# The last block of an output projection's weights, fetched row by row at the end of a decode kernel

## The chip, the cores and the metric

One core of a Trainium2 chip. The metric is the time of one execution on the device in microseconds (us), the median of several; lower is better. The trace's own clock starts at the program's first instruction, and its span is some 2 us shorter than the time.

## The reference

A decode step for 4 sequences. Part A is attention of one query over a cache of 8192 keys and values with 32 heads, then an output projection by `wo`; part B is a gated MLP on the one token of each sequence. The two are mixed by a gate.

```python
q = (x @ wq).reshape(B, Sq, H, Dh) ...
scores = einsum("bhqd,bhkd->bhqk", q, k_cache) * (Dh ** -0.5)
o = einsum("bhqk,bhkd->bhqd", softmax(scores), v_cache)
a = o ... .reshape(B, Sq, H * Dh) @ wo          # wo: 4096 x 1024, bf16
b = x + (silu(x @ w_gate) * (x @ w_up)) @ w_down * sigmoid(x @ w_r)
return g * a + (1 - g) * b                      # 4 x 1 x 1024
```

575.68 MB are read from HBM, nearly all of it the two caches. `wo` is 8.4 MB of that, and nearly all of it comes last.

## The kernel before

The caches stream through a ring of buffers. `wo` comes in 8 blocks, 0 to 7, each 128 partitions by 4 rows of 1024 columns (1 MB); blocks 0 and 1 are issued just ahead of the last value caches, blocks 2 to 7 behind all of them. `wo_block` issues one piece's transfer at once and returns `use`, which emits the matmuls of that piece later. Each row needs two matmuls, one for each half of the columns; all add into the same two accumulators.

```python
def mm_acc(n, lhsT, rhs, start=False):                     # L286 in the profile is its matmul
    nc.tensor.matmul(acc(n), lhsT=lhsT, rhs=rhs, start=start, stop=True, ...)

def wo_block(g, r0=0, r1=FR, half=None):                   # FR = 4 rows, NH = 2 halves, NB = 512
    ...
    if half is None:                                       # L394
        nc.sync.dma_start(out=w[:, r0:r1]..., in_=wov[:, g, r0:r1]...)
    else:                                                  # L397
        nc.sync.dma_start(out=w[:, r0, half * NB:(half + 1) * NB], in_=...)
    def use():
        for r in range(r0, r1):
            for n in range(NH) if half is None else [half]:
                mm_acc(n, LT[:, r, g, :], w[:, r, n * NB:(n + 1) * NB])
    return use
# ... the end of the program; NWB = 8:
last = [wo_block(g) for g in range(2, 4)]
cuts = [(g, r, r + 2) for g in range(4, NWB) for r in (0, 2)][:-1] \
       + [(NWB - 1, 2, 3)] + [(NWB - 1, 3, 4, n) for n in range(NH)]
last += [wo_block(*cut) for cut in cuts]                   # all transfers issued here, in this order
flush_sums(); last.pop(0)(); flush(); flush_late(); last.pop(0)()
o_rows(GE, NWB)
for use in last:                                           # matmuls of blocks 4 to 7
    use()
nc.vector.tensor_copy(out=res[0], in_=acc(0))              # L636
nc.sync.dma_start(out=out2[:, 0:NB], in_=res[0])           # L637
nc.scalar.copy(out=res[1], in_=acc(1))                     # L638
nc.scalar.dma_start(out=out2[:, NB:D], in_=res[1])         # L639
```

## Time and profile before

| | before |
|---|---|
| time, median of 3 runs (lowest to highest) | 1343.54 us (1343.23 to 1343.93) |
| span in the profile | 1341.3 us |
| PE busy | 1052.3 us (78%) |
| DVE busy | 638.3 us (48%) |
| DMA engines, mean rate | 430 GB/s, full in 39 of 40 slices |

How to read it: no compute engine is full, the DMA engines are. PE is the TensorE, DVE the VectorE, ACT the ScalarE, SP the engine that issues most transfers. A transfer runs on 16 DMA engines here, and each adds one to the transfer's semaphore when its share is through: the sixteenth increment is what this text calls the landing. Only the end, where the transfers have run out and the last matmuls, copies and output transfers follow, is free to be shortened by order alone.

### The profile page before, as it was taken

The page shows a single profiled execution, that of the slowest core. Times are in us where ns is not written, and L with a number is a line of the kernel's source. Part 1 is how long each engine was busy: PE and PEld are TensorE (multiplying, and loading weights), DVE is VectorE, ACT ScalarE, POOL GpSimd, SP SyncE. Part 2 cuts the span into 40 slices and gives each one's busy share as a digit, 9 for nine tenths or more (in the row PEclk, how much of TensorE's full clock was granted, in tenths as well). Part 3 has the DMA queues.
Part 4 walks back from the last instruction along what each step waited for, and adds up shares of the span by engine and source line. Part 5 has one row for each costly group of instructions (what it writes and reads, how often), then busy time and mean ns, then how long its engine had stood idle before and what let it go on. Part 6 is the DMA issues. An engine that isn't in the chain of part 4 may idle for free.

```text
span 1341.3 us, 6870 instructions
## 1 busy us (share of the span) xinstructions
PE 1052.3 (78%) x4550; PEld 138.5 (10%) x1396; DVE 638.3 (48%) x386; ACT 66.2 (5%) x99; POOL 71.5 (5%) x209
## 2 busy tenths in 40 slices
PE   2565877887778788787879778789597879888888
PEld 0000000001001010001001010101011011111111
DVE  2555988556544347454436256646145556100000
ACT  0000000200000000100000000100000000111000
POOL 2000000100000001000000000100000000100000
PEclk9777989898988898888899888889898889889989
DMA  9999999999999999999999999999999999999998
GB/s 415 436 432 436 435 436 424 441 430 427 435 436 427 442 434 420 441 430 433 437 431 432 430 436 434 436 428 427 434 431 439 434 421 441 434 422 432 426 427 337
DMA packets 15322, 576.13 MB, mean 430 GB/s; under 512 B 1710, under 2 KB 1974, under 8 KB 3004
## 3 DMA queue, kind: packets, MB, share of 16 engines
q1 hardware_dynamic: 15284, 575.69, 99.6%
q8 instruction: 23, 0.38, 0.1%
q14 instruction: 7, 0.06, 0.0%
q10 hardware_dynamic: 8, 0.00, 0.0%
HBM read 575.68 MB, written 0.01 MB: 429 GB/s over the span
## 4 chain that ended last, share of the span: by engine, by line
DMA 67%; DVE 21%; PE 11%; issue 0%; ACT 0%; SPq 0%; DVEq 0%
DMA ring<-in_A_k_cache_dram 51%; DVE TB L456 19%; PE o_ps L540 8%; DMA ring<-in_A_v_cache_dram 7%; DMA ring<-in_A_wo_dram 6%; PE S_ps L461 3%; DMA ring<-in_B_w_gate_dram 3%; DVE OS L561 2%; PE o_ps L320 0%; DVE PT L497 0%; DVE mx L483 0%; PE acc L286 0%; PE led L577 0%; PE o_ps L577 0%; DVE OS L569 0%
## 5 line engine op out<-in xcount | busy, mean ns | idle before, releaser
L456 DVE STREAM_TRANSPOSE TB<-ring 128x2048 uint32<-128x2048 uint32 x256 | 568.3, 2278 | 472.5 <-DMA ring<-in_A_k_cache_dram 464.5
L461 PE MATMUL S_ps<-TB,Z 128*128 128x512 bf16 x1990 | 526.3, 415 | 197.3 <-DVE TB L456 183.0
L540 PE MATMUL o_ps<-ring,PB 128*64 128x512 bf16 x2048 | 462.9, 388 | 50.4 <-DMA ring<-in_A_v_cache_dram 49.0
L461 PEld LDWEIGHTS <-Z 128*128 128x128 bf16 x512 | 53.2, 104 | 655.5 <-issue 655.5
L540 PEld LDWEIGHTS <-PB 128*64 128x64 bf16 x512 | 57.2, 112 | 449.6 <-issue 446.9
L516 POOL COPY PB<-PT 32x256 bf16<-32x256 bf16 x64 | 38.9, 608 | 712.5 <-PE o_ps L540 519.6
L569 DVE SCALAR_TENSOR_TENSOR OS<-o_ps,mE,OS 128x512 f32<-128x512 f32 x5 | 3.8, 751 | 139.2 <-ACT OS L567 139.2
L514 ACT COPY PB<-PT 32x256 bf16<-32x256 bf16 x64 | 39.6, 619 | 257.2 <-PE o_ps L540 251.4
L438 POOL COPY Z<-qa 32x4 bf16<-32x4 bf16 x128 | 25.7, 200 | 460.0 <-PE S_ps L461 432.4
L557 ACT ACTIVATE OS<-o_ps,mE 128x512 f32<-128x512 f32 x11 | 7.6, 687 | 450.3 <-PE o_ps L540 450.3
L561 DVE SCALAR_TENSOR_TENSOR OS<-o_ps,mE,OS 128x512 f32<-128x512 f32 x33 | 24.3, 737 | 1.5
L492 ACT ACTIVATE TB<-S_ps,mx 128x2048 bf16<-128x2048 f32 x4 | 7.9, 1967 | 331.6 <-DVE mx L489 331.6
L286 PE MATMUL acc<-ring,hT 128*4 128x512 bf16 x56 | 14.8, 433 | 5.4 <-ACT TB L492 5.4
L244 PE MATMUL S_ps<-identb,x 6*128 6x6 bf16 x8 | 0.6, 197 | 22.4 <-DMA x<-in_gate_w_dram 22.4
L286 PE MATMUL acc<-ring,LT 128*4 128x512 bf16 x64 | 15.1, 378 | 1.8 <-DMA ring<-in_A_wo_dram 1.3
L577 PEld LDWEIGHTS o_ps<-selg,OS 128*128 128x128 f32 x88 | 11.5, 191 | 9.3 <-issue 8.9
L497 DVE STREAM_TRANSPOSE PT<-TB 128x2048 bf16<-128x2048 bf16 x4 | 9.2, 2311 | 6.4 <-ACT TB L492 6.4
L483 DVE TENSOR_REDUCE mx<-S_ps 128x1 f32<-128x2048 f32 x4 | 9.1, 2282 | 6.2 <-PE S_ps L461 6.2
L320 PE MATMUL o_ps<-ring,xw 128*4 128x512 bf16 x112 | 9.1, 448 | 3.6 <-DMA ring<-in_B_w_gate_dram 3.6
L577 PE MATMUL o_ps<-selg,OS 128*128 128x8 f32 x88 | 10.5, 245 | 0.0
L567 ACT ACTIVATE OS<-o_ps,mE 128x512 f32<-128x512 f32 x5 | 3.4, 687 | 129.0 <-PE o_ps L540 129.0
L589 DVE SCALAR_TENSOR_TENSOR OT<-led,sgb,rinv 128x8 bf16<-128x8 f32 x5 | 1.2, 236 | 16.4 <-PE led L577 16.4
(73 smaller groups left out, 83.1 us busy)
## 6 DMA issues: line engine op xcount, KB each, us to landing
ring<-in_A_v_cache_dram SPq DMA_DIRECT2D x18, 4096.0 KB, 31.0
ring<-in_A_k_cache_dram SPq DMA_DIRECT2D x14, 4096.0 KB, 30.2
ring<-in_A_v_cache_dram SPq DMA_DIRECT2D x6, 2048.0 KB, 39.4
ring<-in_B_w_gate_dram SPq DMA_DIRECT2D x1, 7168.0 KB, 37.1
ring<-in_B_w_up_dram SPq DMA_DIRECT2D x1, 7168.0 KB, 37.1
ring<-in_B_w_down_dram SPq DMA_DIRECT2D x1, 7168.0 KB
ring<-in_A_wo_dram SPq DMA_DIRECT2D x4, 1024.0 KB
ring<-in_A_v_cache_dram SPq DMA_DIRECT2D x4, 1024.0 KB, 25.8
```

The source lines that it names most:

```text
L286: nc.tensor.matmul(acc(n), lhsT=lhsT, rhs=rhs, start=start, stop=True, skip_group_check=True)
L320: nc.tensor.matmul(ps[32 * k:32 * k + Bn, z, :], lhsT=xT[TW * half + t], rhs=cols(w, t, 4 * z + k), start=(half + t == 0), stop=(half == 1 ...
L438: nc.gpsimd.tensor_copy(out=Z[at, :, QP - 1 + QP * q], in_=qa[at, :, h0 + q, b])
L456: nc.vector.transpose(out=flat_t.bitcast(U32).rearrange("p (j i) -> p j i", j=CJ), in_=kn[:, half].bitcast(U32))
L461: nc.tensor.matmul(sps[:, z, :], lhsT=Z[:, 2 * half + e, s:s + P], rhs=T[:, 16 * z:16 * z + 16, :, e], start=(t + n + half + e == 0), stop ...
L483: nc.vector.tensor_reduce(out=mx[:, 0:1], in_=sps[:].rearrange("p z n -> p (z n)"), axis=AX.X, op=ALU.max)
L497: nc.vector.transpose(out=PT[:].rearrange("p j i -> p (j i)"), in_=PTs)
L514: nc.scalar.copy(out=Bv[at, :, :, q, :], in_=Pv[at])
L516: nc.gpsimd.tensor_copy(out=Bv[at, :, :, q, :], in_=Pv[at])
L540: nc.tensor.matmul(o_ps[w // 2][row:row + NM, w % 2, :], lhsT=PB[:, RD * (d % NW) + n, z].rearrange("p w s j -> p (w s j)"), rhs=vn[:, j0 ...
L561: nc.vector.scalar_tensor_tensor(out=OS[:], in0=o_ps[w // 2][:, w % 2, :], scalar=mE[:, w:w + 1], in1=OS[:], op0=ALU.mult, op1=ALU.add)
L577: nc.tensor.matmul(oT, lhsT=OS[:, q * Dh:(q + 1) * Dh], rhs=selg[:, q].rearrange("p t s -> p (t s)"), start=(q == 0), stop=(q == 3), skip_ ...
```

## The change

The intent: PE should find less work waiting for it when the last bytes have landed. Rows 0 and 1 of block 7 no longer come in one transfer of 512 KB, but as two of 256 KB. Row 2, and row 3 in two halves of its columns, came in pieces of their own before and do so still.

```diff
-    cuts = [(g, r, r + 2) for g in range(4, NWB) for r in (0, 2)][:-1] + [(NWB - 1, 2, 3)] + [(NWB - 1, 3, 4, n) for n in range(NH)]
+    cuts = [(g, r, r + 2) for g in range(4, NWB - 1) for r in (0, 2)] + [(NWB - 1, r, r + 1) for r in range(FR - 1)] + [(NWB - 1, 3, 4, n) for n in range(NH)]
```

## The prediction

> **What bounds the kernel now.** The page's strips over 40 slices come first, and of them the strip of the DMA engines with the rate below it.
>
> ```profile
> DMA  9999999999999999999999999999999999999998
> GB/s 415 436 432 436 435 436 424 441 430 427 435 436 427 442 434 420 441 430 433 437 431 432 430 436 434 436 428 427 434 431 439 434 421 441 434 422 432 426 427 337
> ```
>
> The DMA engines are full in 39 of 40 slices, at some 430 GB/s, and only the last slice falls, to 337 GB/s. 575.68 MB have to be read, and the change reads the same bytes. So nothing the change does can touch the 1330 us ahead of the end; it can only touch the run-out. The chain of waits of the last 20 us says what the run-out hangs on:
>
> ```profile
> 1325.23 11.30 DMA ring<-in_A_wo_dram
> 1336.53 0.04 issue
> 1336.57 1.90 PE acc L286 x8
> 1338.47 0.02 issue
> 1338.49 0.58 ACT TB L638
> ```
>
> One DMA, issued at 1325.23 and landed at 1336.53, is the last thing that the program waits for. The kernel's text says which: the wo blocks are numbered 0 to 7, each of 4 rows of 1024 columns on 128 partitions; blocks 4, 5 and 6 come in two DMAs of two rows (512 KB), block 7 as rows 0-1 (512 KB), row 2 (256 KB), and row 3 in two halves of its columns (128 KB each). The order of issue makes the DMA of 1325.23 rows 0-1 of block 7. After it landed the TensorE does all 8 matmuls of block 7 in one go. Its timeline from 1334 us on:
>
> ```profile
> 1334.06 1.02 PE L286 MATMUL acc<-ring,LT 128*4 128x512 bf16 x4 [0.22 <-DMA ring<-in_A_wo_dram]
> 1335.31 1.02 PE L286 MATMUL acc<-ring,LT 128*4 128x512 bf16 x4 [0.23 <-DMA ring<-in_A_wo_dram]
> 1336.57 1.89 PE L286 MATMUL acc<-ring,LT 128*4 128x512 bf16 x8 [0.23 <-DMA ring<-in_A_wo_dram]
> ```
>
> The two groups of 4 belong to the two DMAs of block 6. They need 1.02 us and then stand idle 0.22 to 0.23 us for the next 512 KB: here the DMA is the slower one. The 8 of block 7 have no idle time inside: the smaller pieces after rows 0-1 had all landed by the time that PE came to them, so over the last 1.9 us PE is the slower one. What follows hangs on the end of it:
>
> ```profile
> 1338.27 0.68 DVE L636 CAST TB<-acc 4x512 bf16<-4x512 f32 x1 [7.84 <-PE acc L286]
> 1338.49 0.58 ACT L638 CAST TB<-acc 4x512 bf16<-4x512 f32 x1 [13.01 <-PE acc L286]
> 1338.98 0.29 SPq L637 DMA_DIRECT2D out_dram<-TB  x1
> 1339.10 0.55 ACTq L639 DMA_DIRECT2D out_dram<-TB  x1
> ```
>
> The right half of the output (ACT's copy, ACT's DMA) is the later one by 0.12 us, so the last matmul, and not the one before it, sets the end; the span ends at 1341.3.
>
> Last, the DMA view of the window 1323 to 1338 shows how the transfers run out:
>
> ```profile
> DMA  9999999999999999999999999976556554544200
> GB/s 393 459 404 404 404 437 426 415 382 382 404 426 404 415 404 404 426 393 426 404 404 404 410 385 391 350 287 262 243 229 246 227 235 183 208 175 164 85 8 0
> ```
>
> From about 1332.5 on only some half of the 16 DMA engines still have work, at 160 to 290 GB/s together. The increments of the semaphores in the trace give the same picture: the first of the 16 engines is through with rows 0-1 of block 7 at 1331.53, the last at 1336.53. Seven engines are ahead, nine lag by 3 to 5 us, and the laggards alone set each landing.
>
> **What the Trainium skill says.** "DMA: Bandwidth & Descriptors", section "Why a DMA increments its semaphore by 16 and not by 1", says that only the full 16 means that all data has landed. The trace agrees: PE starts 0.04 us after the sixteenth increment (1336.53 to 1336.57), 5 us after the first. The same page, section "Measured (HBM→SBUF, 128 partitions, SWDGE, issued from GpSimd)", has the rule to batch DMAs to 1 MiB or more for 75% of peak. That would speak against smaller pieces[...]. These pieces stand one behind another in a queue, and there the trace does not show the loss: sixteenth increments of the last five DMAs are at 1335.27, 1336.53, 1337.17, 1337.51 and 1337.83, so 512 KB took 1.26 us, 256 KB 0.64, 128 KB 0.34 and 0.32. "TensorE: Matmul & The Clock Gate", section "Back-to-back issue gap", gives N/2.4 + 2.5 ns for a warm matmul, 215.8 ns at N = 512. The trace agrees: 8 matmuls less 4 are 1.89 - 1.02 = 0.87 us, 0.217 each, and starts lie 0.215 apart.
>
> **The change part by part.** It replaces one DMA of 512 KB (rows 0-1 of block 7, 4 KB to a partition) by two of 256 KB (2 KB to a partition). Row 2 and the two halves of row 3 were in such pieces before, and stay so. Compared instruction by instruction, PE, DVE, ACT and POOL have the same work in the same order; SP has one DMA more; and PE waits five times in block 7 instead of four, with the first wait for row 0 alone.
>
> *On SP:* one more issue, 0.33 us, with a wait of 0.02. Each DMA here waits until the one eight places before it has landed. Row 0 of block 7 keeps the place of the old piece (1325.23); each later piece moves one place back: row 1 to 1327.72, row 2 to 1329.00, row 3's left half to 1330.28, and its right half gets the place after the first DMA of block 5, whose sixteenth increment is at 1331.49, so 1331.55. The lagging engines come to that piece at 1337.5, six microseconds later: off the path. The seven fast ones come to it at about 1332.6; an output DMA took 1.1 us from issue to its first data landing (1338.98 to 1340.12), so they may stand idle for a few tenths. They have 5 us to spare.
>
> *On the DMA engines:* the pieces of block 7 follow the landing at 1335.27. With 0.64 for each 256 KB: row 0 at 1335.91, row 1 at 1336.55, row 2 at 1337.19, row 3 left at 1337.53, right at 1337.85. That is 0.02 later at the end than before (2 x 0.64 against 1.26). A less kind reading: the packets of 4, 2 and 1 KB took a mean of 159, 84 and 46 ns late in the run, so 16 of 2 KB for 8 of 4 KB are 1.34 us against 1.27, or 0.07 more.
>
> *On PE:* block 6's last matmul starts at 1335.95, so PE is free at 1336.17. Row 0 is there by then: two matmuls, 1336.17 and 1336.38, in time that was idle or waiting. Row 1: landed 1336.55, starts 1336.60 and 1336.81. Row 2: landed 1337.19, plus 0.04, starts 1337.23 and 1337.45. Row 3: left free to go at 1337.66 (landed 1337.53), right at 1337.89 (landed 1337.85, plus 0.04). Before, the last matmul started at 1338.07. **Gain 0.18 us**; with the less kind packets the right half lands at about 1337.90 and the gain is 0.13.
>
> *The cap:* the last piece landed at 1337.83 before, and PE could not have begun on it ahead of 1337.87. However rows 0-1 are cut, no more than 1338.07 - 1337.87 = 0.20 us is to be had, since the cut moves matmuls ahead of the last landing and does not move the landing. What comes behind (copies, output DMAs, 3.2 us from 1338.07 to the end) shifts along unchanged.
>
> The sum: 2 matmuls that no longer stand between the last landing and the end would be 0.43 us, of which 0.20 was exposed, less some 0.04 for more packets and one more wait: 0.16 us, 0.012% of the time. 1343.54 - 0.16 = 1343.38.
>
> **The rivals.** First, *the landing takes the place of PE as the bound and eats all of it*: if small packets cost more than the packet means say, say 0.2 us for 16 of them, the end stays at 1343.5. For it: PE's slack on the last landing is only 0.20. Against it: 256 KB took 0.64, as good as half of 512 KB. Second, *the later issue starves the queue*: were the lagging engines to run dry, each gap of over 1 us would go straight to the end, giving 1344.5 or more. Against it: 6 us between issue and use on those engines. Third, *the gain is twice mine*: if the transfers of the laggards ran faster once the others are done sooner, or if the wait at 1337.19 vanished, 1343.1. Against it: between the landings the laggards needed 1.25 us (1334.02 to 1335.27) with half of the engines idle and 1.29 with all at work, so hardly faster. Fourth, *the noise is larger than any of these*: the three runs of before lie between 1343.23 and 1343.93, 0.70 us apart, four times the gain. This I hold for the likeliest thing to be seen in the times; the gain should be seen in the trace alone.
>
> **The range and the chances.** The middle is 1343.38. The mechanism gives 0 to 0.2 us; the spread of before is 0.35 to each side of its middle, and another set of runs can lie a few tenths off as a whole, for which I widen to 1342.5 and 1344.2. For 2% the time would have to move by 27 us, and the change has its hands on the last 16 us only: within 2% 0.99, the rest split evenly, for a run in a slower state.
>
> **What would show it.** Right: in the last 5 us of the changed kernel, PE's 8 matmuls come no longer in one group, but in two or three, with waits of hundredths to 0.25 us; row 0's two follow block 6 with no wait; the last matmul starts 2.62 to 2.7 us after the last landing of block 6 (2.80 us before, from 1335.27 to 1338.07); five DMAs of block 7. Wrong: a landing of the last piece more than 2.7 us after block 6's; a gap in the queue of the lagging engines; PE's last group still of 8, or a change anywhere ahead of 1325 us.

## The result, and the profile after

The changed kernel took 1343.21 us (median of 6 runs, 1342.81 to 1344.05), the kernel before 1343.43 us in its own 6 (1343.09 to 1343.93). The ratio of the fast runs is 0.9999, 95% interval 0.9986 to 1.0011: the same within 2%, and no difference clear of noise. The prediction said 1343.38 in a range of 1342.5 to 1344.2, and the median lies inside. That alone shows little: the median of the kernel before (1343.43) lies inside as well.

The chain of waits at the end of the changed kernel (start in us, duration, what) answers to the one before:

```profile
1328.86 8.22 DMA ring<-in_A_wo_dram
1337.08 0.04 issue
1337.12 1.04 PE acc L286 x4
1338.16 0.02 issue
1338.18 0.57 ACT TB L638
```

The transfer that released PE last is now the one issued at 1328.86, which is row 2 and not rows 0-1, and 4 matmuls stand behind it instead of 8. The timeline of PE, its weight loads (PEld) and the copies shows the rest:

```profile
1335.15 2.99 PE L286 MATMUL acc<-ring,LT 128*4 128x512 bf16 x12 [0.20 <-DMA ring<-in_A_wo_dram]
...
1336.67 0.08 PEld L286 LDWEIGHTS <-LT 128*4 128x4 bf16 x1 [0.35 <-issue]
1337.34 0.08 PEld L286 LDWEIGHTS <-LT 128*4 128x4 bf16 x1 [0.59 <-issue]
1337.96 0.68 DVE L636 CAST TB<-acc 4x512 bf16<-4x512 f32 x1 [7.67 <-PE acc L286]
1338.18 0.57 ACT L638 CAST TB<-acc 4x512 bf16<-4x512 f32 x1 [12.84 <-PE acc L286]
1338.67 0.29 SPq L637 DMA_DIRECT2D out_dram<-TB  x1
1338.79 0.55 ACTq L639 DMA_DIRECT2D out_dram<-TB  x1
```

The 12 matmuls in one group are the four of block 6's second piece and all of block 7. The view runs them together although there is a wait inside: the ends of matmuls are modelled and overlap the next start, so a short wait leaves hardly any idle time to print. The weight loads give it away. One load stands ahead of every two matmuls, and the pause between two loads is 0.35 us when PE streams; ahead of the load at 1337.34 it is 0.59. The 0.24 us more are PE waiting for row 2: its first matmul starts at 1337.12, 0.04 us after the landing at 1337.08 (chain above).

To compare executions, one offset must come out first. The moment at which block 6's last piece has landed differs from one execution to the next by more than the change is worth: 1335.06 to 1336.13 us over the 13 profiles in the table below. So I count from that landing. It is the sixteenth increment of that transfer's semaphore, as the trace records it; starts of single matmuls and the last landing are from the trace too. The three columns after the first are differences.

| run | block 6 landed | last piece of block 7 landed, after that | last matmul started, after that | last start to end of span | time of this profiled run |
|---|---|---|---|---|---|
| before | 1335.27 | 2.57 | 2.81 | 3.25 | 1343.33 |
| changed | 1335.11 | 2.62 | 2.66 | 3.19 | 1342.88 |
| after_again | 1335.25 | 2.61 | 2.72 | 3.20 | 1343.18 |
| whole | 1335.18 | 2.45 | 4.00 | 3.45 | 1344.59 |
| rows4 | 1335.69 | 2.58 | 2.93 | 3.25 | 1343.94 |
| extra_early | 1335.19 | 2.61 | 2.93 | 3.19 | 1343.31 |
| extra_late | 1335.25 | 2.61 | 2.96 | 3.19 | 1343.37 |
| before_late | 1335.16 | 2.56 | 3.89 | 3.25 | 1344.16 |
| after_late | 1335.06 | 2.61 | 3.64 | 3.20 | 1343.93 |
| before_early | 1335.32 | 2.57 | 2.81 | 3.25 | 1343.24 |
| after_early | 1335.94 | 2.61 | 2.66 | 3.17 | 1343.62 |
| early_gap | 1336.13 | 2.62 | 2.66 | 3.16 | 1343.81 |
| halves_early | 1335.31 | 2.68 | 2.72 | 3.39 | 1343.44 |

The last matmul starts 0.15 us sooner after block 6's landing (2.81 to 2.66). The fourth column holds a second gain, of 0.06 us, that I had not foreseen. At the end SP waits for each transfer semaphore in turn, in a fixed order, two to an instruction. The count of such instructions from the last landing on, in the view of that line for the kernel before, the changed kernel and the run whole:

```profile
L665 SPq EVENT_SEMAPHORE  x2: 28/28/28, 1340.4 to 1340.5; - x2
```

```profile
L665 SPq EVENT_SEMAPHORE  x1: 28/28/28, 1340.1 to 1340.1; - x1
```

```profile
L665 SPq EVENT_SEMAPHORE  x5: 28/28/28, 1341.5 to 1341.8; - x5
```

The semaphores of the transfers are taken in rotation. The one transfer more moves the last output transfer to the semaphore that SP comes to last, so that one wait instruction is left after its landing and not two; in whole there are five. One such step takes 0.06 to 0.07 us in the trace (1341.54, 1341.61, 1341.68, 1341.74, 1341.81 in whole). 0.15 + 0.06 make 0.21 us, on these profiles. The medians are 0.22 apart, but with runs of one kernel spread over 1.2 us that agreement is luck and proves nothing; the gain is seen in the trace, not in the times.

### The profile page after: what moved, and what is told of

The parts are those of the page before. It is cut to its first block, busy times and chain, and to the rows that moved or that the text cites. A ratio compares the mean times of both kernels' runs of the same rounds, so it can differ in the third digit from the quotient of the medians.

```text
span 1341.0 us, 6872 instructions
## 1 busy us (share of the span) xinstructions
PE 1050.9 (78%) x4550; PEld 138.3 (10%) x1396; DVE 638.2 (48%) x386; ACT 66.2 (5%) x99; POOL 71.4 (5%) x209
## 4 chain that ended last, share of the span: by engine, by line
DMA 62%; DVE 24%; PE 12%; another core or an unknown queue 1%; issue 0%; ACT 0%; SPq 0%; DVEq 0%
DMA ring<-in_A_k_cache_dram 51%; DVE TB L456 21%; PE o_ps L540 9%; DMA ring<-in_A_v_cache_dram 7%; DMA ring<-in_A_wo_dram 2%; DVE OS L561 2%; DMA x<-in_gate_w_dram 2%; PE S_ps L461 1%; PE acc L286 1%; DVE mx L483 0%; PE S_ps L320 0%; PE led L577 0%; PE o_ps L320 0%; DVE PT L497 0%
```

## The experiments

Theory: the end is set by the later of two things, PE's stream of matmuls and the landings on the lagging DMA engines; the cut takes matmuls from behind a landing, and wins at most what PE stood behind the last landing before. Rivals: the cut does nothing and the last landing alone counts; the cut costs as much as it wins; PE sets the end anyway.

### The changed kernel again, and three other cuts

The diffs of this part and of the last one show the cuts against the changed kernel, shortened with `...`.

**after_again**: no edit.

> The changed kernel once more, on the same chip as the three below. Theory (PE stood behind the landing of rows 0-1; the cap is the last landing): the profile again has 2.6 to 2.7 us from the sixteenth increment of block 6's last DMA to the start of the last matmul (2.80 in the kernel before, 2.66 in the changed one), and the median lies 0.1 to 0.3 us under the kernel before, not clear of noise. Rival (the 2.66 was a chance of one profile): 2.75 or more this time.

Measured: median 1343.1 us (5 runs), the kernel before 1343.33 (9 runs), ratio 0.9999 (0.9986 to 1.0011). In the profile the last start came 2.72 us after block 6's landing: just outside what I expected, and nearer to the rival. The reason is in the timeline of PE:

```profile
1331.49 6.85 PE L286 MATMUL acc<-ring,LT 128*4 128x512 bf16 x31
```

31 matmuls without a pause up to the end: here PE did not wait for any piece of blocks 4 to 7. It came late to them, its first matmul of block 4 being at 1331.28 and not at 1329.82. The time was lost about 1290 us. The stretch 1280 to 1300 us by engine (busy us and instructions of PE, PEld, DVE, ACT, POOL, then the granted TensorE clock, which is the share of its full speed that PE was allowed, the busy share of the DMA engines, and GB/s), with the value-cache matmuls that follow, for the kernel before and then for after_again:

```profile
1280.00:1300.00 20.00, 14.37 (x63) 2.48 (x21) 2.34 (x4) 1.27 (x2) 0.00 (x0) 0.83 1.00 424
```

```profile
1292.81 12.27 PE L540 MATMUL o_ps<-ring,PB 128*64 128x512 bf16 x56
```

```profile
1280.00:1300.00 20.00, 14.39 (x51) 3.12 (x18) 2.34 (x4) 1.26 (x2) 0.00 (x0) 0.74 1.00 424
```

```profile
1293.54 14.16 PE L540 MATMUL o_ps<-ring,PB 128*64 128x512 bf16 x56
```

The granted clock was 0.74 there and not 0.83, and the same 56 matmuls took 1.9 us more. The DMA engines moved the same 424 GB/s. So in some executions PE is in time, and in others late. In after_again the last piece landed 2.61 us after block 6; PE could have begun on it at 2.65, and began at 2.72 because it was busy. That PE's place decides is tested further down.

**whole**: block 7 in one transfer.

```diff
-    cuts = ... + [(NWB - 1, r, r + 1) for r in range(FR - 1)] + [(NWB - 1, 3, 4, n) for n in range(NH)]
+    cuts = ... + [(NWB - 1, 0, FR)]
```

> Block 7 in one DMA of 1 MB. Theory: the last landing stays where it is (2.5 to 2.6 us after block 6's), but all 8 matmuls then stand behind it, so the last one starts 2.55 + 0.04 + 7 x 0.2155 = 4.1 us after block 6's landing, against 2.66 in the changed kernel and 2.80 before: the median 1.4 us over the changed kernel, 1.3 over the kernel before, clear of noise. Rival (the end follows the landing of the last bytes alone, the cut does nothing): the median within 0.2 us of the changed kernel.

Measured: median 1344.59 us (5 runs), 1.49 over after_again on the same chip and 1.26 over the kernel before; the ratio to the kernel before is 1.0012 (0.9999 to 1.0026), which just touches 1. The timeline of PE:

```profile
1335.22 1.02 PE L286 MATMUL acc<-ring,LT 128*4 128x512 bf16 x4 [0.22 <-DMA ring<-in_A_wo_dram]
1337.67 1.89 PE L286 MATMUL acc<-ring,LT 128*4 128x512 bf16 x8 [1.43 <-DMA ring<-in_A_wo_dram]
```

PE stands idle for 1.43 us and then has all 8 matmuls before it. The last start is 4.00 us after block 6's landing (4.1 expected). Block 7 itself landed sooner than in any other cut, at 2.45 us, and the time is the longest of the table: the rival, that the end follows the landing alone, falls. Of the 1.6 us that its profile lies above the changed kernel's from block 6's landing to the end, 1.34 are the matmuls and 0.26 the four further closing waits.

**rows4**: the four rows, row 3 not halved.

```diff
-    ... + [(NWB - 1, r, r + 1) for r in range(FR - 1)] + [(NWB - 1, 3, 4, n) for n in range(NH)]
+    ... + [(NWB - 1, r, r + 1) for r in range(FR)]
```

> Block 7 row by row, its last row not halved (the row part of the change without the halves). Theory: two matmuls stand behind the last landing and not one, the landing itself 0.02 to 0.04 us earlier for fewer packets: the last matmul starts 2.60 + 0.04 + 0.22 = 2.86 us after block 6's landing, 0.2 over the changed kernel and 0.06 over the kernel before. Rival (the halves win nothing, for their packets cost what they save): 2.66.

Measured, one look: last landing 2.58, last start 2.93, so 0.07 over what I expected, and 0.27 over the changed kernel's first profile. PE was late in this execution as well (clock 0.74 in the same stretch, no pause from 1331.93 on), so the excess is PE's own lateness: it could have begun row 3 at 2.62, began at 2.72, and row 3's second matmul is 0.22 behind. The landing is level with that of four pieces in the kernel before. But with PE streaming to the end, halves of row 3 would not have moved the last start: its 2.93 is block 7's first start, 1.42 after block 6's landing, plus seven matmuls (1.51). So this run doesn't tell what the halves are worth, and the rival (the halves win nothing) stays untested; by an estimate from the landing, with PE in time the last start would have come at 2.58 + 0.04 + 0.22 = 2.84.

**seven**: an attempt to shorten the lag itself, by giving rows 2-3 to seven of the DMA engines only. I took these seven to be the ones that are ahead.

```diff
+    def wo_seven(g, r0, r1):
+        for lo, hi in ((0, 119), (119, 126), (126, 128)):
+            nc.sync.dma_start(out=w[lo:hi, r0:r1]..., in_=wov[lo:hi, g, r0:r1]...)
+    ...
-    ... + [(NWB - 1, r, r + 1) for r in range(FR - 1)] + [(NWB - 1, 3, 4, n) for n in range(NH)]
+    ... + [(NWB - 1, 0, 1)] + [(NWB - 1, 1, 2, n) for n in range(NH)]
+    # rows 2-3 of block 7 by wo_seven: issued ahead of block 6, used after block 5's first piece
```

> Rows 2-3 of block 7 in transfers of 119, 7 and 2 partitions[...], issued ahead of block 6; rows 0 and 1 as before, row 1 now the one in halves; PE takes rows 2-3 after the first piece of block 5. Theory (the end is the lag of nine engines; the seven that are ahead are the lowest-numbered): the laggards have 0.65 x 2 us less to do, the last landing comes 1.3 us after block 6's and the last matmul 1.3 to 1.7 after it, the median 1.0 us under the changed kernel, 1342.2. Rival (the seven that are ahead are others): several of the lowest seven are laggards, get 2.9 us of rows 2-3 for the 1.3 they lose, and the median is 1.2 to 1.8 us over the changed kernel, with block 6's landing late. A second rival (the lag does not matter, all engines share one rate): no change in the median.

Measured: median 1350.72 us (5 runs), ratio to the kernel before 1.005 (1.0037 to 1.0062). That is 7.6 us over after_again, much worse than even the first rival had it. The profiled run took 1348.12, the shortest of the five, so the profile holds 4.9 of the 7.6 us at most. Its PE timeline, and two stretches by engine in it and in the changed kernel:

```profile
1338.69 4.48 PE L286 MATMUL acc<-ring,LT 128*4 128x512 bf16 x20 [3.38 <-DMA ring<-in_A_wo_dram]
```

```profile
1326.00:1332.00 6.00, 5.30 (x28) 1.71 (x17) 2.34 (x4) 1.27 (x2) 0.00 (x0) 1.00 0.95 295
```

```profile
1326.00:1332.00 6.00, 5.96 (x48) 2.15 (x35) 1.32 (x4) 0.00 (x0) 0.00 (x0) 1.00 1.02 406
```

The transfer of 119 partitions did run on seven engines: its semaphore shows seven late increments, from 1331.7 to 1338.4. At least three of the seven are therefore laggards, and my assumption that this shape would pick the seven engines that are ahead falls. PE waited 3.38 us for these rows and then had 20 matmuls before it. There is more: from 1326 us on the DMA engines moved 295 GB/s where the changed kernel had 406, while busy for 95% of the time. On the lagging engines, the ordinary pieces of 512 KB ahead of it landed 1.97 and 2.20 us apart (sixteenth increments 1332.09, 1334.06, 1336.26) instead of 1.28. These slow steps begin as the first engines come to the transfer of 119 partitions (they were through with the piece ahead of it at 1327.73). So it seems to have slowed others that were not behind it in a queue; one profile shows this in time, and by what path no run here shows.

### Is PE in the way or not

**extra_early** and **extra_late**: one idle matmul into a bank that nobody reads any more, between rows 1 and 2 of block 7, or between rows 2 and 3.

```diff
-    for use in last:
+    for n, use in enumerate(last):
         use()
+        if n == len(last) - 4:          # - 3 in extra_late
+            nc.tensor.matmul(A_ps[1][0:Bn, 0], lhsT=LT[:, 0, 0, :], rhs=wo_home[1][:, 0, 0, 0:NB], start=True, stop=True, ...)
```

> The changed kernel with one idle matmul (0.2155 us, into a bank nobody reads) between rows 1 and 2 of block 7. Theory: where PE is not late, it stood idle about 0.24 us at that place, waiting for row 2, so the matmul is free: the last matmul 2.66 us after block 6's landing, at most 0.02 more. If this execution has PE late (no idle time from 1331 us on, as the second profile of the changed kernel and rows4 had after a dip of the granted clock to 0.74 between 1280 and 1300 us), it costs its full 0.22. Rival (PE sets the end even where it shows idle time): 2.88 with an idle gap still there.

> The same idle matmul one row later, between row 2 and row 3. Theory: behind row 2's landing PE and the last landings are level (both gave 1337.77 in the first profile), so it costs its full 0.22: 2.88 us after block 6's landing, or 2.7 + 0.22 = 2.94 if PE is late. Rival (the last landing alone sets the end): 2.66.

Measured, one look each: 2.93 and 2.96. Both executions had the clock at 0.74 about 1290 us and PE late, without a pause from 1331.4 and 1331.5 on. In that state both cost about a full matmul over after_again's 2.72 (0.21 and 0.24), as expected for a late PE. But extra_early could not answer its question in this state; that is done below.

**before_late** and **after_late**: 8 idle matmuls (1.7 us) ahead of block 4, in both kernels, so that PE is late whatever the clock.

```diff
     o_rows(GE, NWB)
+    for _ in range(8):
+        nc.tensor.matmul(A_ps[1][0:Bn, 0], lhsT=LT[:, 0, 0, :], rhs=wo_home[0][:, 0, 0, 0:NB], start=True, stop=True, ...)
     for use in last:
```

> The kernel before with 8 idle matmuls (1.7 us) ahead of block 4, which make PE late on purpose. Theory: PE has no idle time from there to the end, so the place of the cut can't matter: the last matmul starts 31 x 0.2155 = 6.68 us after the first of block 4's, and 3.6 to 4.0 us after block 6's landing. Rival (the landing of rows 0-1 still holds the 8 last ones back): an idle gap ahead of block 7.

> The changed kernel with the same 8 idle matmuls. Theory: the same as the kernel before with them, 6.68 us from the first matmul of block 4 to the last start, no idle time, and the gain of 0.14 us gone (the two apart by less than 0.03 in this measure). Rival (the cut wins even so): 6.5 or less.

PE's timeline in before_late and in after_late:

```profile
1332.36 7.07 PE L286 MATMUL acc<-ring,LT 128*4 128x512 bf16 x32
```

```profile
1332.00 7.07 PE L286 MATMUL acc<-ring,LT 128*4 128x512 bf16 x32
```

The 32 matmuls of blocks 4 to 7 take 7.07 us in both, without a pause; from the first start to the last it is 6.69 us in both (1332.36 to 1339.05, 1332.00 to 1338.69). The two profiles differ after block 6's landing (3.89 and 3.64) by nothing but where PE stood when it began. So with PE late the place of the cut does not matter, and the gain of the matmuls is gone. The gain in the closing waits stays (3.25 and 3.20).

**before_early**, **after_early** and **early_gap**: the 8 matmuls of wo block 3 left out, so that PE is early whatever the clock. The result is wrong (it still lay within the comparison's tolerance). early_gap is after_early with the idle matmul of extra_early.

```diff
     flush_late()
-    last.pop(0)()
+    last.pop(0)
     o_rows(GE, NWB)
```

> The kernel before without the 8 matmuls of wo block 3 (its data still arrives; the result is wrong on purpose), so that PE is 1.7 us ahead and waits for the wo data whatever the clock did before. Theory: as in the profile of the kernel before, the 8 matmuls of block 7 in one group after the landing of rows 0-1, the last one 2.78 to 2.82 us after block 6's landing. Rival (the 2.80 came from that execution's PE): 2.7 or less.

> The changed kernel with the same cut in PE's work. Theory: 2.64 to 2.68 us from block 6's landing to the last start, a gap of about 0.24 us ahead of row 2, and 0.12 to 0.16 less than the kernel before in the same state. Rival (the gain needs more than PE being in time): 2.75 or more, or no gap.

> The changed kernel with PE early and one idle matmul between rows 1 and 2: extra_early again, where PE was late and so could not answer. Theory: the idle time there is real and takes the 0.22 us, so 2.64 to 2.70. Rival (PE sets the end throughout): 2.85 or more.

PE's timeline in before_early, after_early and early_gap:

```profile
1335.36 1.02 PE L286 MATMUL acc<-ring,LT 128*4 128x512 bf16 x4 [0.23 <-DMA ring<-in_A_wo_dram]
1336.62 1.89 PE L286 MATMUL acc<-ring,LT 128*4 128x512 bf16 x8 [0.23 <-DMA ring<-in_A_wo_dram]
```

```profile
1335.99 2.99 PE L286 MATMUL acc<-ring,LT 128*4 128x512 bf16 x12 [0.20 <-DMA ring<-in_A_wo_dram]
```

```profile
1336.17 1.90 PE L286 MATMUL acc<-ring,LT 128*4 128x512 bf16 x8 [0.23 <-DMA ring<-in_A_wo_dram]
1337.91 0.38 PE L636 MATMUL led<-ring,LT 128*4 128x512 bf16 x1
1338.13 1.04 PE L286 MATMUL acc<-ring,LT 128*4 128x512 bf16 x4
```

2.81 and 2.66 again: the gain of 0.15 us comes back when PE is in time. In early_gap the idle matmul at 1337.91 lies just ahead of row 2's at 1338.13, and the last start is at 2.66 all the same. The wait that the weight loads showed is real, and a matmul put into it is free.

### Cutting finer

**halves_early**: block 7 in eight pieces, PE early as above.

```diff
-    ... + [(NWB - 1, r, r + 1) for r in range(FR - 1)] + [(NWB - 1, 3, 4, n) for n in range(NH)]
+    ... + [(NWB - 1, r, r + 1, n) for r in range(FR) for n in range(NH)]
```

> Block 7 in eight pieces of 128 KB (each row in two halves), PE early as above; three more issues than the change, each later piece issued one to three places later. Theory (packets cost hundredths, issue is far ahead of use on the lagging engines): the last landing 2.60 to 2.72 us after block 6's, the last start 0.04 after it, 2.64 to 2.76; nothing more to win. Rival (each further DMA costs 0.1 us or more, or the lagging engines run dry): the last landing at 2.9 or later, with gaps between the pieces' landings of over 0.4 us.

Measured: last landing 2.68, last start 2.72, with 0.31 to 0.37 us between the landings of the eight pieces. Each of the last four starts follows its landing by 0.04 to 0.06. The lagging engines do not run dry, though the last piece was issued as late as 1335.38. The issue is not the limit, and neither is PE; what is left is a cost of each further piece, of its packets as I take it, and the finer cut loses 0.06 us in landing. Its closing waits come out worse too (3.39). So none of the cuts tried is clearly better than the kernel as changed.

Set side by side, the landing of block 7 after block 6's grows with the number of pieces: 2.45 us in one, 2.57 in the four of the kernel before, 2.62 in five, 2.68 in eight. That is 0.03 us for each piece more (0.23 over seven).

## Why the prediction was right

- **Only the run-out can be touched.** Right. Block 6 landed at 1335.27 before and 1335.11 after, which lies within the spread of executions.
- **PE stood behind the landing of rows 0-1, with 8 matmuls.** Right, where PE is in time: 2.81 twice (before, before_early). I took that state for the only one. after_again, rows4, extra_early and extra_late found PE late, and before_late and after_late show that this part of the gain is then nothing if PE is late enough. How much is left between depends on how late PE is. An estimate: the kernel before can't start block 7 before rows 0-1 have landed, 1.26 + 0.04 = 1.30 us after block 6, and then needs 1.51 us to the last start, 2.81. In after_again PE came to block 7 at 1.21 and was at its last start at 2.72, so 0.09 would be left; in rows4 it came at 1.42, and nothing would be. So the 0.15 us is what the executions with PE in time give, not the mean of all.
- **Row 0 goes into idle time, PE then waits for row 2, and the last start is 2.62 to 2.7 after block 6's landing.** Right: 2.66 in the changed kernel and in after_early. The wait ahead of row 2 was 0.24 us in the trace, where my schedule (1336.81 to 1337.23 for two starts 0.2155 apart) left 0.20.
- **Two packets for one cost 0.02 to 0.07 us.** Right: the last landing went from 2.57 to 2.62, 0.05.
- **The later issue is off the path.** Right; halves_early pushed it 4 us further and the laggards still did not run dry.
- **The cap of 0.20 us.** The whole of it could not be had, since the landing moved by 0.05; 0.15 was. I had 0.16 in the sum (0.20 less 0.04).
- **"What comes behind shifts along unchanged."** Wrong by 0.06 us: the last output transfer took another semaphore, and one closing wait less followed it. It is small, but nearly four tenths of the gain foreseen, and the same effect costs whole 0.26 us.
- **The noise is larger than the gain.** Right. The landing of block 6 alone varies by 1.07 us between executions. Six runs a side leave the ratio open from 0.9986 to 1.0011, which is 1.9 us down and 1.5 us up; a gain of 0.2 us can't be told from times here. That the median fell so near the number is luck.

What stays open: how often PE is late. The clock's dip and PE's lateness go together in the profiles looked at (0.74 and late in after_again, rows4, extra_early and extra_late; 0.83 or more and in time in before, changed and whole), and the slower matmuls lie in the same stretch. What makes the clock dip longer there in some executions than in others was not tested.

What makes nine of the DMA engines lag I did not test either, but the traces point to it. Beside the data, the DMA engines carry the program's own instructions. In the DMA view of the kernel before (queue, kind: packets, MB, share of the 16 engines):

```profile
q8 instruction: 23, 0.38, 0.1%
q14 instruction: 7, 0.06, 0.0%
```

Each of the 23 is one packet of 16 KB and took 0.94 to 1.11 us, where a packet of 16 KB of data took 0.62 (1300 to 1326 us). The lags can be read from the semaphores, in transfers with all 16 increments on record. In the transfer whose first increment is at 38 us, no other is over 1 us behind it; at 462 us, after eight of the 23 packets, nine are; at 927 us, after 16, nine are over 2.5 us behind. From one such transfer to the next, the lags of all 16 together grow by a median of 1.53 us where one of the 23 packets lies between, and by 0.09 where none of either kind does; in the other 13 traces it is 1.43 to 1.56, against -0.07 to 0.06. This is an agreement in time, in every trace; no run took the packets away, and which engine carried one is not in the trace. The lag is worth more than the cut: at 1329 us the 16 lags had a mean of 2.75 us and a longest of 5.06, so shared evenly they would let the last piece land some 2.3 us sooner (an estimate).

## What to carry to other kernels

At the end of a transfer-bound kernel, ask which is later: the last landing, or the queue of work behind the landing before it; cutting the last pieces wins what the work stands behind, and no more, here 0.15 us for four pieces made five and 1.3 us for the step from one piece to five. A gain that small is read from the trace, from one event in the run to another, because the offsets between executions are larger; and look at more than one execution, since a change of the granted clock can hand the bound to another engine. Work of no use, put into an idle gap or ahead of it, tells cheaply whether the gap is real and who sets the end. And where some DMA engines lag, look for what else they carry before cutting finer.

## What the Trainium skill lacked or had wrong

- "DMA: Bandwidth & Descriptors" (section "Measured (HBM→SBUF, 128 partitions, SWDGE, issued from GpSimd)") advises batches of 1 MiB, by a table of transfers issued from GpSimd. It doesn't say what cutting costs where pieces issued from SP stand one behind another in a queue: here 1 MB landed 2.45 us after the piece ahead of it in one piece, and 2.68 in eight of 128 KB.
- No page that I read has nine of the 16 DMA engines of a core fall behind the other seven, or ties such a lag to transfers of instructions: in the kernel before the first was 5.0 us ahead of the last on the same transfer (1331.53 and 1336.53), and the landing went by the last. While only the laggards had work, the transfers ran at 160 to 290 GB/s. The lags grew with the 23 instruction packets, by some 1.5 us for each.
- "DMA: Bandwidth & Descriptors" (section "Why a DMA increments its semaphore by 16 and not by 1") takes the number of engines of a transfer from the size of its slowest dimension, which is the partitions here, and the run seven agrees for 119 partitions (seven increments). It doesn't say what such a shape costs the others: 295 GB/s instead of 406 in the same 6 us, and 2.0 to 2.2 us instead of 1.28 for ordinary pieces of 512 KB queued ahead of it.
- "TensorE: Matmul & The Clock Gate" (section "Back-to-back issue gap") gives a sustained spacing of about 131 ns for matmuls of 512 columns in a real kernel, and calls the 216 ns of its formula an over-count. Here a stream of 32, with a weight load ahead of every two, ran at 216 ns (6.69 us over 31): in this stream the formula holds and the 131 does not.
- No page has the cost of the closing waits: SP steps through the transfer semaphores in a fixed order at 0.06 to 0.07 us an instruction, so which semaphore the last output transfer happened to use was worth up to 0.26 us here.
